# Dummy matmuls moved into the gaps of a fill, and one GpSimd addition put behind a sum: attention and gated FFN on one core

## The chip, the core and the metric

One core of a Trainium2 chip. The metric is the device time of one execution in microseconds; the time before is the median of five runs, 349.6 us. TensorE (PE) multiplies, VectorE (DVE), ScalarE (ACT) and GpSimd (POOL) work on what it leaves in PSUM and on SBUF; SyncE (SP) and GpSimd issue the DMAs. PSUM has eight banks, here one array `ps` of 128 x 8 x 512 fp32 values.

## What is computed

Hourglass attention over 8 batches x 8 heads, 576 positions, 64 per head, and then a gated FFN over the 4608 tokens:

```
q_d, k_d, v_d = means of q, k, v over 4 neighbouring positions
out_d  = softmax(scale * q_d k_d^T) v_d            # 144 x 144
local  = softmax(scale * q k^T where |i-j| < 4) v  # band of width 7
x      = repeat(out_d, 4) + local                  # 4608 tokens x 512
out    = (relu(x w_gate) * (x w_val)) w_out        # 512 -> 1536 -> 512
```

Inputs and output are fp32; the kernel computes in fp16 and sums in fp32.

## The kernel before, in words

Two heads make a pair; there are 32 pairs. The attention of a pair consists of its loads (q, k and v, cast to fp16 by POOL's DMAs), transposes of q and k, scores in 128-column blocks of the band and for the pooled keys, exponentials, masks, products with v, and a normalised sum into `xT`. The FFN takes 512 tokens at a time: `hg` and `hv` are the products with w_gate and w_val (four matmuls of 512 columns each, L639), `relu` (ACT) and `gate` (DVE) make `gT`, and the product with w_out is done by steps `p1` to `p7` (L724), a Strassen-like scheme that needs four sums of parts of `gT` on DVE (`sums`, L718: s1, s2, s3, s4; the 128-wide part `sumhi`, the rest `next`, and whole ones by `sum`). The last sum of an output unit is s4.

The order on each engine is written out by hand in three lists of tokens. `FRONT` is the fill: the first pairs are transposed on PE (`tr`, L364) and copied out (`ev`, by ACT or DVE, L378), v is pooled by PE (`vd`, L408, copied by `vc`), the scores are `s1` (L427, L438), their exponentials `ed` and `ex` (ACT), masks `ma` (DVE, L454), products `sd` (L475) and `su` (L487), the normalising steps on DVE `rd`, `td` (L504), `ru`, `tu` (L518), and the transposition into `xT` `xp` (L622, L624) with its copy `xe`. The last number of a token is its PSUM bank: `td/0/6` reads bank 6, and `ev/1/01A/7` reads bank 7. Loads are tokens too, so their place in the list is their place in POOL's queue. `ORDER` is one period of the body: four pairs and one FFN chunk; a token such as `v2/b/0` is kind, argument, half. `TAIL` ends the kernel without attention.

In the body POOL pools v: `v4` is the DMA load, `emit_v2` (L386) adds halves of it into an fp32 tile, `emit_v1` (L392) adds halves of that into `vd`. The step `after` (L994) copies one column of s4 to a scrap tile `seen`: POOL's queue stops there until that sum is done. It stands once in a period, as `after/3/0`. Transposes of q and k in the body are DMAs of SP (L344), issued with `scores`, followed by a reduction on DVE (L351).

`emit_warm` issues matmuls of zeros whose result nobody reads. Before, twelve of 512 columns come first (bank 7), and two groups of two, 248 columns each, in bank 6.

Of the kernel before, what the change touches and what calls it, by code (L numbers as in the profile page):

```python
# [16 lines left out]

FRONT = """
pads loadk/0 loadv/0 loadq/1 loadk/1 loadv/1 loadq/2 cast tr/0/2/4 loadk/2 ev/0/20V/4 tr/0/1/3
tr/0/0/2 ev/0/21V/4 ev/0/10A/3 vd/0/6 loadv/2 ev/0/11A/3 ev/0/01A/2 ev/0/00A/2 loadq/3 warm/2  # L20
tr/1/0/7 vc/0/6 s1/0/2 ev/1/00A/7 loadk/3 tr/1/2/1 ed/0/2 tr/1/1/0 ev/1/20V/1 ev/1/11A/0 loadv/3
sd/0/6 ev/1/21V/1 ev/1/10A/0 rd/0/6 ex/0/0/2 td/0/6 wg/0 warm/2 vd/1/6 ev/1/01A/7 ma/0/0
ex/0/1/2 s1/1/0 wv/0 ma/0/1 ed/1/0 ones/4 su/0/4 ex/1/1/0 ru/0/4 loadq/4 ex/1/0/0 tu/0/0/4
tr/2/1/2 tr/2/2/3 tu/0/1/4 ev/2/11A/2 tr/2/0/0 ev/2/10A/2 loadk/4 ev/2/21V/3 xp/0/0/4 ev/2/20V/3
ev/2/01A/0 xp/0/1/5 ev/2/00A/0 ma/1/0 loadv/4 vc/1/6 s1/2/0 ma/1/1 xe/0/0A/4 xe/0/1V/5 sd/1/6
ex/2/1/0 ones/5 su/1/4 rd/1/6 td/1/6 ed/2/0 ru/1/4 vd/2/6 loadq/5 tu/1/1/4 ex/2/0/0 tr/3/1/2
tu/1/0/4 tr/3/2/3 loadk/5 vc/2/6 tr/3/0/0 ev/3/20V/3 ev/3/10A/2 xp/1/1/5 sd/2/6 ev/3/21V/3
loadv/5 ev/3/01A/0 xe/1/1V/5 xp/1/0/4 ev/3/00A/0 ma/2/0 ev/3/11A/2 ma/2/1 xe/1/0A/4 s1/3/0 wg/1
rd/2/6 su/2/4 td/2/6 ed/3/0 ru/2/4 ex/3/0/0 tu/2/1/4 hv/0/0/7 wv/1 hv/0/1/7 tu/2/0/4 ex/3/1/0
vd/3/6 ma/3/0 ones/6 xp/2/1/5 vc/3/6 xp/2/0/4 ma/3/1 sd/3/6 xe/2/1V/5 xe/2/0A/4 loadq/6 tr/4/0/0  # L30
rd/3/6 su/3/4 td/3/6 tr/4/1/2 loadk/6 ru/3/4 hv/1/0/1 ev/4/11A/2 tu/3/0/4 hg/0/0/6 ev/4/10A/2
hg/0/1/6 tu/3/1/4 loadv/6 tr/4/2/3 ev/4/01A/0 ev/4/00A/0 xp/3/1/5 ev/4/21V/3 ev/4/20V/3 xp/3/0/4
wg/2 hv/0/2/7 xe/3/1V/5 xe/3/0A/4 hg/1/0/0 s1/4/2 wv/2 hv/0/3/7 ex/4/0/2 hv/1/1/1 loadq/7
# [75 lines left out]
ORDER = """  # L109
p/1/0 gate/5/1< scores/a/0 keep/1/0 gate/4/1< hg/0/0 exp/a0/0 sumhi/0/0 sumhi/1/0 exp/a1/0  # L110
hv/0/0 mask/a0/0 ed/a/0 mask/a1/0 p/2/0 next/0/1< relu/0/0 next/1/1< o/a00/0 o/a01/0 c11//0
o/a10/0 ln/a0/0 o/a11/0 sum/2/0 p/6/0 v/a/1 sum/3/0 p/5/0 keep/2/0 pool/b/0 v2/b/0 ln/a1/0 p/7/0
hg/2/0 keep/3/0 after/3/0 v1/a/1 inv/a/0 c22//0 p/4/0 gate/0/0 v2/a/0 p/3/0 xn/a1/0 c21//0 relu/2/0 hg/1/0
xn/a0/0 qk/a0/1 hv/2/0 relu/1/0 qk/a1/1 c12//0 xsum/a/0 scores/b/0 qk/a2/1 next/0/0 hv/1/0
exp/b0/0 v/b/0 exp/b1/0 hg/4/0 mask/b0/0 gate/1/0 v4/a/1 ed/b/0 hg/3/0 mask/b1/0 relu/4/0
gate/2/0 v1/b/0 o/b00/0 o/b01/0 o/b10/0 pool/a/0 ln/b0/0 o/b11/0 hv/4/0 v2/a/1 ln/b1/0 hv/3/0
# [53 lines left out]
def kernel(  # L170
# [34 lines left out]
    keep = ctx.enter_context(tc.tile_pool(name="keep", bufs=1))  # L205
# [15 lines left out]
    def ring(n, shape, dtype, name):  # L221
        return [keep.tile(shape, dtype, name=f"{name}{i}") for i in range(n)]
# [8 lines left out]
    v2 = [t[0:72] for t in v2full]  # L231
# [5 lines left out]
    ed = ring(2, [72, 2, 2 * SD + 64], FP16, "ed_")  # L237
    vd = ring(3, [72, 2, 192], FP16, "vd_")
# [3 lines left out]
    xn = keep.tile([128, 2, 360], FP16, name="xn")  # L242
# [7 lines left out]
    ps = psum.tile([128, 8, 512], FP32, name="ps")  # L250
# [45 lines left out]
    def emit_load_q1(hp, i):  # L296

        b, off = head_off(hp)
        src, dst, hh = (q, k)[i // 2], qk16[hp % NL][:, i // 2, :], i % 2
        if hp < NTP:  # L300
            if hh:
                return
            first = hp == 0 and src is q
            (nc.sync if first else nc.gpsimd).dma_start(
                (q32 if first else dst).rearrange("p (n d) -> p n d", d=64),
                _dap(src, off, [[D, 96], [NQ * D, 2 * NB], [1, D]]),
            )
            return
        nc.gpsimd.dma_start(  # L309
            dst.rearrange("p (j h d) -> p j h d", h=2, d=64)[:, :, hh, :],  # L310
            _dap(src, off + hh * S * D, [[D, 96], [NQ * D, NB], [1, D]]),
        )
# [182 lines left out]
    rd = ring(2, [72, 2, 2], FP32, "rd_")  # L495
    ru = ring(2, [96, 2, NB], FP32, "ru_")
# [310 lines left out]
            _dap(moe_w_out, 384 * i * D_MODEL, [[D_MODEL, 128], [128 * D_MODEL, 3], [1, D_MODEL]]),  # L807
        )

    def emit_warm(n, wide=False):  # L810
        for _ in range(n):
            nc.tensor.matmul(
                out=ps[:, 7, :] if wide else ps[:, 6, 264:512],
                lhsT=zero_sb[:, 0:128],
                rhs=zero_sb[:, 128 : 640 if wide else 376],
                start=True,
                stop=True,
            )
# [114 lines left out]
    def emit_tail_step(kind, arg, at):  # L933
        c, j = (int(at[0]), int(at[1])) if len(at) == 2 else (int(at or 0), 0)
        i = int(arg[0]) if arg else 0
        if kind in ("hg", "hv"):
            w = int(kind == "hv")
            bank = 4 + i if w else 2 * (j % 2) + i
            emit_h_mm(c, j + NK * i, w, range(4), ps[:, bank, :])
        elif kind == "relu":  # L940
            emit_relu(2 * j + i, ps[:, 2 * (j % 2) + i, :])
        elif kind == "gate":
            emit_gate(c, j + NK * i, 2 * j + i, ps[:, 4 + i, :])
        elif kind in ("gateg", "gateb"):
            nc.vector.scalar_tensor_tensor(
                out=gT[c % 2][:, j + NK * i, :],
                in0=block(c, j, 0).t[i],
                scalar=0.0,
                in1=ps[:, 4 + i, :] if kind == "gateg" else block(c, j, 1).t[i],
                op0=ALU.max,  # L950
                op1=ALU.mult,
            )
        elif kind == "xs":
            emit_xs(c, i)
        elif kind == "wg":
            emit_ws(0, i, 0, 768, nc.vector)
        elif kind == "wv":
            emit_ws(1, i, 192 * int(arg[1]), 192 * int(arg[1]) + 192, nc.gpsimd)
        elif kind in ("qg", "qv"):
            block(c, j, int(kind == "qv")).q(i)  # L960
        elif kind in ("keepg", "keepv"):
            block(c, j, int(kind == "keepv")).keep(i - 1)
        elif kind in ("tg", "tv"):
            block(c, j, int(kind == "tv")).out(arg)
        elif kind == "part":
            lo, hi = ((0, 3), (3, 5), (5, 6))[int(arg[1])]
            unit(c, j).sums(lo, hi, (i,))
        else:
            UNIT_STEPS[kind](unit(c, j), i)

    def emit_step(kind, arg, u, c):

        banks = (u, 1 - u)
        i = int(arg[-1]) if arg and arg[-1].isdigit() else 0
        if kind in H_STEPS:
            pp, jj = banks[i % 2], 6 * u + i
            if kind == "relu":
                emit_relu(i, pair(pp)[:, 0, :])
            elif kind == "gate":
                emit_gate(c, jj, i, pair(pp)[:, 1, :])  # L980
            else:
                w = int(kind == "hv")
                emit_h_mm(c, jj, w, range(4), pair(pp)[:, w, :])
        elif kind in UNIT_STEPS:
            UNIT_STEPS[kind](unit(c - 1, u), i)
        elif kind == "next":
            w = unit(c - 1, 1) if u == 0 else unit(c, 0)
            w.sums(0, NK if u == 0 else 5, (i,))
        else:
            PAIR_STEPS[kind](4 * c + 2 * u + LEAD + "ab".index(arg[0]), arg[1:])  # L990
# [45 lines left out]
    def emit_periods(c0, c1):  # L1036
        for base in range(c0, c1 + 2):
            for tok in ORDER.split():
                c = base + {">": 1, "<": -1}.get(tok[-1], 0)
                kind, arg, u = tok.rstrip("<>").split("/")  # L1040
                if c == c1 - 1 and base > c:
                    continue
                if c0 <= c < c1 or c == c0 - 1 and f"{kind}/{arg}/{u}" in LATE:
                    emit_step(kind, arg, int(u), c)

    def emit_front(tok):
        kind, *a = tok.split("/")
        if "@" in tok:
            emit_step(kind, a[0], *map(int, a[1].split("@")))
        else:  # L1050
            FRONT_STEPS[kind](*[int(x) if x.isdigit() else x for x in a])

    FRONT_STEPS = {
        "pads": emit_pads,
        "cast": lambda: nc.scalar.copy(out=qk16[0][:, 0, :], in_=q32),
        "warm": emit_warm,
        "loadq": lambda p: emit_load_q1(p, 0),
        "loadk": lambda p: emit_load_q1(p, 2),
# [37 lines left out]
    with tc.manual_schedule(engines={ET.PE, ET.DVE, ET.Activation, ET.SP, ET.Pool}):  # L1096
        nc.scalar.dma_start(cst_sb[:, 960:1080], cst_dr[:, 960:1080])
        emit_load_q1(0, 0)
        nc.sync.dma_start(cst_sb[:, 0:960], cst_dr[:, 0:960])
        nc.sync.dma_start(cst_sb[:, 1080:1368], cst_dr[:, 1080:1368])  # L1100
        emit_warm(12, True)
        for tok in FRONT.split():
            emit_front(tok)
        emit_periods(PS // 4, (NP - LEAD) // 4)
        for tok in TAIL.split():
            kind, arg, *at = tok.split("/")
            if at:
                emit_tail_step(kind, arg, at[0])
            else:
                emit_step(kind, arg, 1, NCH - 3)  # L1110
# [30 lines left out]
```

## Time and profile before

| | us |
|---|---|
| median of 5 runs | 349.6 |
| lowest, highest | 347.19, 351.98 |
| profiled execution, its own time | 349.6 |
| its span, first to last instruction | 347.8 |

The mean granted TensorE clock of the profiled execution is 0.979 of full. In the page, a row of digits gives 40 equal slices of the span, 8.7 us each, with the busy share in tenths; PEclk is the granted clock in tenths. In a timeline a row gives start, length, engine, line, operation and tiles, xN for N merged instructions, and in brackets the idle time before it with what ended it. In a table by stage, each engine's busy microseconds are followed by its number of instructions. [...]

### The profile page before, as it was taken

What the parts mean: (1) busy time and instruction counts of PE and PEld (TensorE: products, weight loads), DVE (VectorE), ACT (ScalarE), POOL (GpSimd) and SP (SyncE); (2) the same over time, 40 slices, a digit from 0 to 9 for tenths busy, and PEclk for the clock granted to TensorE, in tenths of its full rate; (3) what the DMA queues carried; (4) which work ended last, traced back from release to release, by engine and by line L of the source; (5) the groups of instructions that cost most, each with busy time, mean ns of one, the idle gap of its engine ahead of it and who ended that gap; (6) DMA issues with size and microseconds to landing.
All of it is one profiled execution on the core that took longest, in us unless ns stands there. A gap on an engine that the chain in (4) does not pass through costs nothing.

```text
span 347.8 us, 8224 instructions
## 1 busy us (share of the span) xinstructions
PE 339.2 (98%) x3210; PEld 218.1 (63%) x3210; DVE 296.3 (85%) x546; ACT 218.5 (63%) x423; POOL 182.2 (52%) x232
## 2 busy tenths in 40 slices
PE   7799999999999999999999999999999999999996
PEld 3676555757566655665566656665666557767685
DVE  5566659999899999999999999999999798786892
ACT  3766876777766776767667765776767634344222
POOL 8986547796789894977587696950300000000000
PEclk9759999999999999999999999999999999999999
DMA  9999999999999999799969995992000001001023
GB/s 145 165 170 187 185 189 154 151 177 148 148 170 156 140 163 142 95 141 151 150 75 144 164 152 62 156 151 70 30 32 33 30 0 47 32 31 47 32 74 108
DMA packets 167975, 40.02 MB, mean 115 GB/s; under 512 B 149857, under 2 KB 164865, under 8 KB 167937
## 3 DMA queue, kind: packets, MB, share of 16 engines
q0 software_dynamic: 132160, 22.63, 93.4%
q1 hardware_dynamic: 35632, 16.84, 27.7%
q8 instruction: 25, 0.41, 0.5%
q14 instruction: 14, 0.11, 0.1%
q10 hardware_dynamic: 144, 0.03, 0.1%
HBM read 45.86 MB, written 9.44 MB: 159 GB/s over the span
## 4 chain that ended last, share of the span: by engine, by line
PE 88%; DVE 5%; DMA 2%; ACT 2%; issue 1%; POOL 1%; DVEq 0%; ACTq 0%; POOLq 0%
PE ps L639 46%; PE ps L724 22%; PE ps L905 4%; PE ps L585 3%; PE ps L438 2%; PE ps L427 2%; PE ps L364 2%; DMA qk<-in_k_dram 2%; PE ps L593 2%; PE ps L408 1%; DVE xn L612 1%; ACT rden L603 1%; DVE ee L454 1%; DVE xo L718 1%; PE ps L622 1%
## 5 line engine op out<-in xcount | busy, mean ns | idle before, releaser
L639 PE MATMUL ps<-xT,wv_sb 128*128 128x512 f16 x432 | 109.5, 380 | 0.0
L639 PE MATMUL ps<-xT,wg_sb 128*128 128x512 f16 x352 | 88.4, 380 | 0.0
L648 ACT ACTIVATE r<-ps 128x512 f16<-128x512 f32 x88 | 52.0, 596 | 31.4 <-PE ps L639 28.8
L651 DVE TENSOR_TENSOR gT<-r,ps 128x512 f16<-128x512 f16 x88 | 58.8, 681 | 7.7 <-PE ps L639 4.9
L639 PEld LDWEIGHTS <-wv_sb 128*128 128x128 f16 x432 | 40.5, 98 | 39.7
L639 PEld LDWEIGHTS <-wg_sb 128*128 128x128 f16 x352 | 32.6, 98 | 32.3 <-issue 0.2
L612 DVE TENSOR_TENSOR xn<-ps,rden 64x720 f16<-64x720 f32 x48 | 43.5, 905 | 4.1 <-ACT rden L608 2.7
L603 ACT ACTIVATE rden<-ps 64x720 f32<-64x720 f32 x48 | 36.7, 765 | 14.6 <-PE ps L593 13.5
L448 ACT ACTIVATE ee<-ps 112x576 f16<-112x576 f32 x64 | 38.8, 648 | 6.6 <-PE ps L438 5.6
L309 POOL DMA_DIRECT2D qk<-in_q_dram x46 | 33.6, 735 | 11.5 <-DMA qk<-in_k_dram 3.2
L724 PEld LDWEIGHTS <-gT 128*128 128x128 f16 x324 | 31.5, 98 | 9.0
L454 DVE TENSOR_TENSOR ee<-ee,cst_sb 112x576 f16<-112x576 f16 x64 | 31.9, 519 | 5.8 <-ACT ee L448 5.2
L309 POOL DMA_DIRECT2D qk<-in_k_dram x46 | 33.7, 736 | 4.6 <-DMA v<-in_v_dram 2.2
L334 POOL DMA_DIRECT2D vw<-in_v_dram x30 | 28.7, 955 | 9.2 <-PE ps L724 4.4
L724 PEld LDWEIGHTS <-xo 128*128 128x128 f16 x288 | 27.4, 98 | 7.7 <-DVE xo L718 0.3
L351 DVE TENSOR_REDUCE qkd<-qkT 128x288 f16<-128x1152 f16 x23 | 30.9, 1343 | 0.0
L758 ACT COPY q<-ps 128x256 f32<-128x256 f32 x45 | 16.8, 373 | 21.5 <-PE ps L724 20.7
L724 PE MATMUL ps<-wo_sb,gT 128*128 128x256 f16 x216 | 28.0, 273 | 0.0
L724 PE MATMUL ps<-wt,xo 128*128 128x256 f16 x216 | 27.7, 273 | 0.2 <-DVE xo L718 0.2
L386 POOL TENSOR_TENSOR v<-v 72x512 f32<-72x512 f16 x21 | 25.0, 1190 | 2.8 <-DMA v<-in_v_dram 2.2
L915 ACT COPY vw<-ps 128x256 f32<-128x256 f32 x30 | 10.8, 374 | 20.7 <-PE ps L905 13.8
L571 DVE TENSOR_TENSOR xT<-xn 128x576 f16<-128x576 f16 x28 | 22.8, 814 | 0.5
(108 smaller groups left out, 562.9 us busy)
## 6 DMA issues: line engine op xcount, KB each, us to landing
out_dram<-y_sb SPq DMA_DIRECT2D x24, 256.0 KB, 3.4
vw<-in_v_dram POOLq DMA_DIRECT2D x30, 168.0 KB, 7.0
qk<-in_q_dram POOLq DMA_DIRECT2D x46, 72.0 KB, 6.5
qk<-in_k_dram POOLq DMA_DIRECT2D x46, 72.0 KB, 6.5
v<-in_v_dram POOLq DMA_DIRECT2D x21, 144.0 KB, 7.1
out_dram<-y_sb SPq DMA_DIRECT2D x22, 128.0 KB, 1.7
wg_sb<-in_moe_w_gate_dram POOLq DMA_DIRECT2D x4, 384.0 KB, 10.3
wv_sb<-in_moe_w_val_dram POOLq DMA_DIRECT2D x4, 384.0 KB, 10.9
```

The source lines that it names most:

```text
L309: nc.gpsimd.dma_start(dst.rearrange("p (j h d) -> p j h d", h=2, d=64)[:, :, hh, :], _dap(src, off + hh * S * D, [[D, 96], [NQ * D, NB], [ ...
L334: nc.gpsimd.dma_start(t, _dap(v, base, [[D, WK], [NQ * D, n], [1, D]]))
L351: nc.vector.tensor_reduce(out=qkd[hp % 2].rearrange("p i t -> p (i t)"), in_=qkT[hp % 4][:, 0 : 2 * S].rearrange("p (t f) -> p t f", f=4), ...
L386: nc.gpsimd.tensor_tensor(out=m, in0=t[:, :, 0:128], in1=t[:, :, 128:256], op=ALU.add)
L448: nc.scalar.activation(out=o, in_=ps[0:WK, p0 + 2 * g : p0 + 2 * g + 2, 0:288], func=AF.Exp, scale=scale)
L454: nc.vector.tensor_tensor(out=o, in0=o, in1=_sap(masks_sb, (0, WK), 288 * g, [[0, 2], [1, 288]]), op=ALU.mult,)
L603: nc.scalar.activation(out=rden[lo : lo + 64], in_=ps[de : de + 64, 4 + 2 * hh : 6 + 2 * hh, 0:360], func=AF.Ln)
L612: nc.vector.tensor_tensor(out=xn[lo : lo + 64], in0=ps[lo : lo + 64, 4 + 2 * hh : 6 + 2 * hh, 0:360], in1=rden[lo : lo + 64], op=ALU.mult,)
L639: nc.tensor.matmul(out=out, lhsT=w[:, kk, bass.ts(jj, 128)], rhs=xT[:, kk, c * TCH : (c + 1) * TCH], start=(kk == 0), stop=(kk == 3),)
L648: nc.scalar.activation(out=r1[j % 3], in_=h1, func=AF.Relu)
L651: nc.vector.tensor_tensor(out=gT[c % 2][:, jj, :], in0=r1[j % 3], in1=h2, op=ALU.mult)
L724: nc.tensor.matmul(out=out, lhsT=left[:, i, :], rhs=right[i], start=(first and i == 0), stop=(i == NK - 1), skip_group_check=True,)
```

## The change

Two edits. In the fill the dummies get a bank as a second argument, and there are more of them: 14 wide ones first, then groups of 5, 5, 5, 1, 3 and 4 of 248 columns, in banks 6, 7, 7, 7, 7 and 1. The second group stands behind `vd/1` and the copy of bank 7, where it stood ahead of `vd/1`. In the body `v2/b/0` (one addition of L386 per period) moves from behind `pool/b/0` to behind `after/3/0`. The order of ACT, DVE and SP is the same; on POOL only the addition and the `seen` copy change places, in five periods; PE has 21 more matmuls, with their weight loads.

```diff
 FRONT = """
...
-tr/0/0/2 ev/0/21V/4 ev/0/10A/3 vd/0/6 loadv/2 ev/0/11A/3 ev/0/01A/2 ev/0/00A/2 loadq/3 warm/2
+tr/0/0/2 ev/0/21V/4 ev/0/10A/3 vd/0/6 loadv/2 ev/0/11A/3 ev/0/01A/2 ev/0/00A/2 loadq/3 warm/5/6
 tr/1/0/7 vc/0/6 s1/0/2 ev/1/00A/7 loadk/3 tr/1/2/1 ed/0/2 tr/1/1/0 ev/1/20V/1 ev/1/11A/0 loadv/3
-sd/0/6 ev/1/21V/1 ev/1/10A/0 rd/0/6 ex/0/0/2 td/0/6 wg/0 warm/2 vd/1/6 ev/1/01A/7 ma/0/0
+sd/0/6 ev/1/21V/1 ev/1/10A/0 rd/0/6 ex/0/0/2 td/0/6 wg/0 vd/1/6 ev/1/01A/7 warm/5/7 ma/0/0
 ex/0/1/2 s1/1/0 wv/0 ma/0/1 ed/1/0 ones/4 su/0/4 ex/1/1/0 ru/0/4 loadq/4 ex/1/0/0 tu/0/0/4
-tr/2/1/2 tr/2/2/3 tu/0/1/4 ...
+warm/5/7 tr/2/1/2 tr/2/2/3 tu/0/1/4 ...
-... ma/1/0 loadv/4 vc/1/6 s1/2/0 ma/1/1 ...
+... ma/1/0 loadv/4 vc/1/6 warm/1/7 s1/2/0 ma/1/1 ...
-ex/2/1/0 ones/5 su/1/4 rd/1/6 td/1/6 ed/2/0 ru/1/4 vd/2/6 loadq/5 ...
+ex/2/1/0 ones/5 su/1/4 rd/1/6 td/1/6 ed/2/0 ru/1/4 warm/3/7 vd/2/6 loadq/5 ...
...
-vd/3/6 ma/3/0 ones/6 xp/2/1/5 vc/3/6 ...
+vd/3/6 ma/3/0 ones/6 warm/4/1 xp/2/1/5 vc/3/6 ...
...
 ORDER = """
...
-... keep/2/0 pool/b/0 v2/b/0 ln/a1/0 p/7/0
-hg/2/0 keep/3/0 after/3/0 v1/a/1 inv/a/0 ...
+... keep/2/0 pool/b/0 ln/a1/0 p/7/0
+hg/2/0 keep/3/0 after/3/0 v2/b/0 v1/a/1 inv/a/0 ...
...
-    def emit_warm(n, wide=False):
+    def emit_warm(n, bank=7, wide=False):
         for _ in range(n):
             nc.tensor.matmul(
-                out=ps[:, 7, :] if wide else ps[:, 6, 264:512],
+                out=ps[:, 7, :] if wide else ps[:, bank, 264:512],
                 lhsT=zero_sb[:, 0:128],
                 rhs=zero_sb[:, 128 : 640 if wide else 376],
...
-        emit_warm(12, True)
+        emit_warm(14, wide=True)
```

## The prediction

> **What bounds the kernel now.** I read the page first, then the busy time by stage, then the timelines of TensorE and of VectorE, then the same around GpSimd's `seen` copy.
>
> ```profile
> PE 339.2 (98%) x3210; PEld 218.1 (63%) x3210; DVE 296.3 (85%) x546; ACT 218.5 (63%) x423; POOL 182.2 (52%) x232
> ...
> PE   7799999999999999999999999999999999999996
> ...
> DVE  5566659999899999999999999999999798786892
> ...
> PEclk9759999999999999999999999999999999999999
> ```
>
> PE is full from the third slice (17 us) to the last, and the granted clock is below full in slices two and three alone. From 95 to 237 us I compared each matmul's start with the start before it: what its columns do not explain is 0.97 to 1.6 us in each period of 35.4 us. So the body is bound by PE, and a microsecond won in the fill arrives at the end, if nothing else becomes late. The fill by stage (columns: PE, PEld, DVE, ACT, POOL busy, then the clock and DMA):
>
> ```profile
> 5.60:8.90 3.30, 2.01 (x35) 1.15 (x33) 0.95 (x4) 0.84 (x4) 3.30 (x5) 1.00 2.42 155
> 9.00:12.30 3.30, 2.14 (x50) 1.65 (x51) 1.58 (x5) 3.05 (x9) 3.30 (x5) 1.00 2.43 155
> 12.40:15.70 3.30, 2.80 (x46) 2.42 (x46) 1.49 (x5) 2.01 (x4) 3.30 (x5) 0.50 2.39 160
> 15.80:19.10 3.30, 3.30 (x53) 2.68 (x49) 2.07 (x6) 2.31 (x7) 3.30 (x5) 0.50 1.41 200
> 19.20:22.50 3.30, 3.17 (x47) 2.61 (x45) 2.57 (x7) 2.33 (x7) 2.26 (x4) 0.50 2.24 162
> 22.70:26.00 3.30, 3.30 (x43) 2.38 (x41) 2.34 (x7) 2.09 (x6) 3.30 (x5) 0.50 2.32 163
> 26.10:29.40 3.30, 3.11 (x55) 2.12 (x54) 3.06 (x10) 1.52 (x6) 2.04 (x4) 1.00 1.37 202
> ```
>
> The clock is halved for four equal stretches, from 12.39 to 26.04 us. There PE is busy while DVE and ACT are some 65% busy: the half clock sets the pace. (At the very start the record shows 1.00, but the first dummies stand 427 ns apart, later 512-column matmuls 216 ns: half rate until 5.56.)
>
> ```profile
> 8.51 0.38 PE L812 MATMUL ps<-zero_sb 128*128 128x248 f16 x2
> 9.23 0.40 PE L364 MATMUL ps<-cst_sb,qk 96*64 96x120 f16 x8 [0.34 <-DMA qk<-in_q_dram]
> ...
> 12.09 0.37 PE L812 MATMUL ps<-zero_sb 128*128 128x248 f16 x2 [0.80 <-DVE xo L504]
> 12.30 0.75 PE L408 MATMUL ps<-vw,cst_sb 112*128 112x128 f16 x6
> ...
> 15.20 1.41 PE L364 MATMUL ps<-cst_sb,qk 96*64 96x120 f16 x24 [0.50 <-ACT ee L448]
> ```
>
> The second pair of dummies waits for `td` (they share bank 6), so it comes after the gap that it might have filled.
>
> [...] Weighting each matmul's streaming time by the rows and columns used, I get 0.44 of a full array for 5.56 to 8.97 (clock kept) and 0.34 for 8.97 to 12.39 (clock halved); in the four half-rate windows 0.60, 0.64, 0.64 (not restored) and 0.78 (restored). [...]
>
> **The change part by part.**
>
> *Dummies up to 12.09.* Two more 512-wide ones cost 2 x 0.216 to 0.427, 0.43 to 0.85, inside the wait of 1.27 before the first transposes at 7.41. The first short group grows from 2 to 5 at 0.104 (248 columns): 0.52 from 8.51 to 9.03, inside the wait that ends at 9.23. Both cost nothing; uncovered, they would cost their length.
>
> *Second group.* `vd/1` now comes first: it starts at 12.09 when `td` is done, takes six times 0.056, ends at 12.43; five dummies follow to 12.95 (their bank 7 is free at 12.13, after ACT's copy). So the scores of pair 1 start at 12.98 as before, but at full clock take 0.42 in place of 0.78.
>
> *Third group.* `su/0` needs the masks (13.18) and runs from 13.42 to 13.80; five dummies to 14.32. The transposes of pair 2 wait for ACT: `ed` 0.65 and `ee` 0.55 after the scores, so they start at 14.70, not 15.20. The dummies end inside that wait: 0.50 won.
>
> *From there to 26.6* VectorE sets the pace. Its own rows:
>
> ```profile
> 14.99 1.02 DVE L518 TENSOR_TENSOR xo<-ps,ru 96x384 f16<-96x384 f32 x2
> ...
> 20.13 1.02 DVE L518 TENSOR_TENSOR xo<-ps,ru 96x384 f16<-96x384 f32 x2
> ...
> 25.55 1.02 DVE L518 TENSOR_TENSOR xo<-ps,ru 96x384 f16<-96x384 f32 x2
> ```
>
> Cycles of 5.14 and 5.42. VectorE's work per pair: copies 0.25 + 0.56, masks 0.82, x out 0.46, `rd` 0.18, `td` 0.42, `ru` 0.23, `tu` 1.02: 3.94. At full clock PE delivers each input in time but for small waits: I take 4.17 and 3.95. `tu` then ends at 15.18, 19.35, 23.30 in place of 16.01, 21.15, 26.57: 3.3 us won. The 1, 3 and 4 later dummies (0.10, 0.31, 0.41) lie in PE's waits for ACT and for `td`, `tu`. After 26.04 both run at full clock in the same order, so 3.3 stays. Bounds: 1.9 if the clock is still lost (below), 4.0 if DVE's waits vanish too.
>
> *Loads* must not stop it. In the trace the first w_val slice lands at 21.04 and is first used at 24.99: margin 4.0 against 3.4 won by then; pair 4's q 5.6, the second w_gate slice 5.8, the v of pair 9 5.2, the first DMA transpose 6.2 ahead of its reduction. All hold, the first by 0.6.
>
> *GpSimd's first v addition.* Five times it moves behind `seen`, which already waits for the last sum: no new wait, 1.17 us of work goes from ahead of it to behind it. Behind it stand `v1`, the next `v2`, then q, k, v and v4 loads (each 0.73 to 0.94 of POOL), and with them, through the landed tiles, SP's transposes. All come 1.17 later in periods two to four (in the first `seen` waited for nothing; in the fifth no load follows). POOL then idles 1.07 and 3.02 by 158.8, 1.67 and 1.76 by 195, 2.23 by 229, which takes the delay up, and the transposes land over 6 us ahead. Cost: nothing; without that cover 3 x 1.17 = 3.5. The gain is in one place:
>
> ```profile
> 207.63 1.17 POOL L386 TENSOR_TENSOR v<-v 72x512 f32<-72x512 f16 x1
> 212.15 0.19 POOL L994 COPY seen<-xo 128x1 f16<-128x1 f16 x1 [3.35 <-DVE xo L718]
> ```
> ```profile
> 207.81 1.08 DVE L718 TENSOR_TENSOR xo<-gT 128x128 f16<-128x128 f16 x1
> 208.93 0.22 DVE L718 TENSOR_TENSOR xo<-xo,gT 128x128 f16<-128x128 f16 x1
> ```
>
> A sum of 0.22 took 1.08 beside the addition, and PE lost 0.20 and 0.35 at 209.4 and 210.5 waiting for it. In the other four the addition lay beside work that it slowed by 0.09 or not at all. So 0 to 0.55; behind `seen` it may meet other work, so I take 0.4.
>
> **Sum** against the profiled execution: span 347.8 - 3.3 - 0.4 = 344.1, plus the 1.8 around it: 345.9. That execution took 349.6, which is also the median of the five runs.
>
> **The rivals.** *Clock still lost* (18%). The longest gap, 11.13 to 12.09, gets nothing: the second group is queued behind `vd/1`, which waits for the same `td`. [...] Then vd/1 and the dummies run at half rate, the transposes of pair 2 start 0.9 late at 16.1; but that window holds over 0.8, the clock is back at 15.8, and 8.6 us later (as above from 14.70 to 23.31) stands 24.7 against 26.62: 1.9 won, 347.3. *Loads take it back* (8%): for the small margin of w_val and saturated DMA; against: the other margins. Gain about 1.6: 347.6. *Slower* (8%): the half clock lasts as before, to 26, and dummies are paid at half rate, 0.207 each. Place: 12.4 to 20. Price: scores 0.6 late, the third group 0.5 beyond its wait, 0.4 for the next four: 1.5, with the second edit 350.7. It decides if the window after the loss stays under what restores it; 0.84 against 0.64 speaks against. *POOL's delay reaches PE* (4%): 345.9 + up to 3.5 = 349.4.
>
> **How the numbers follow.** Clock held: 62%, 345.9, own range 344.8 to 347.0. The rest as above. 344.6 to 349.0 leaves out the slower case and a little at each end. About 1% is what a measurement can tell from no change; that bound is 346.1, just above my number, so a little over half of the first case lies below it and, of the others, some hundredths: faster 0.40. Slower (over 353.1) is the slower case with a further loss: 0.06. Same: 0.54.
>
> **What would show it.** Right: clock 1.00 from about 6 to the end, pair 2's transposes near 14.7, `tu` near 19.3 and 23.3, hg's first matmul near 25.5, periods still near 35.4, the 128x128 sums all 0.22. Wrong: a half clock after 12 us, PE waits with a DMA behind them between 22 and 75 us, or PE losing more than 1.6 in a period, waiting for xn, xT or masks slowed by the moved addition.

## The result and the profile after

| | before | with the change |
|---|---|---|
| median, us | 347.43 (77 runs) | 345.79 (40 runs) |
| lowest, highest, us | 345.44, 357.31 | 344.13, 347.74 |
| profiled execution, its span, us | 349.6, 347.8 | 344.8, 343.0 |
| its mean granted clock | 0.979 | 1.000 |

The ratio is 0.9954, 95% interval 0.9939 to 0.9969: faster by about 0.5%, which is within the 1% that the prediction counted as "same". The changed kernel came out where it was forecast (345.9, measured 345.79); the kernel before did not: its median is 347.4, not 349.6, so by the medians 1.6 us were gained and not 3.7. Runs over 1.5% above the fastest of their kernel are left out of the ratio; their clock is not on record here, but in the sets below, where it is, every run of before as long as these had 0.981 or less.

The two profiled executions differ by more than either figure, 4.8 us. The changed one is a good run of its kernel, 1.0 below its median, so it is in part luck that the median met the forecast so closely.

The page of the changed kernel has lost its slow clock:

```profile
PE 336.0 (98%) x3231; PEld 215.9 (63%) x3231; DVE 292.1 (85%) x546; ACT 218.2 (64%) x423; POOL 182.0 (53%) x232
...
PE   8899999999999999999999999999999999999996
...
PEclk9999999999999999999999999999999999999999
```

The same stages as in the prediction, columns as there (PE, PEld, DVE, ACT, POOL, clock, DMA):

```profile
9.00:12.30 3.30, 2.30 (x55) 1.89 (x56) 1.69 (x5) 2.87 (x8) 3.30 (x5) 1.00 2.43 155
12.40:15.70 3.30, 3.03 (x64) 2.36 (x63) 1.99 (x6) 2.26 (x6) 3.30 (x5) 1.00 2.38 161
15.80:19.10 3.30, 3.15 (x76) 2.64 (x75) 3.04 (x9) 3.20 (x9) 3.30 (x5) 1.00 1.34 202
19.20:22.50 3.30, 3.12 (x61) 2.40 (x56) 3.13 (x11) 2.99 (x8) 2.67 (x5) 1.00 2.33 162
```

From 15.8 on VectorE and ScalarE are busy for 3.0 to 3.2 of 3.3 us, where they had 2.1 to 2.6: with the full clock they set the pace. TensorE's timeline shows the groups of dummies (L812) and what follows each:

```profile
7.94 0.69 PE L812 MATMUL ps<-zero_sb 128*128 128x248 f16 x5
9.00 0.40 PE L364 MATMUL ps<-cst_sb,qk 96*64 96x120 f16 x8 [0.37 <-DMA qk<-in_q_dram]
...
11.87 0.49 PE L408 MATMUL ps<-vw,cst_sb 112*128 112x128 f16 x6 [0.80 <-DVE xo L504]
12.20 0.69 PE L812 MATMUL ps<-zero_sb 128*128 128x248 f16 x5
12.82 0.25 PE L427 MATMUL ps<-qkd 64*72 64x144 f16 x2
...
13.71 0.69 PE L812 MATMUL ps<-zero_sb 128*128 128x248 f16 x5
14.67 0.94 PE L364 MATMUL ps<-cst_sb,qk 96*64 96x120 f16 x24 [0.27 <-ACT ee L448]
```

The second group stands between the pooling (L408) and the scores (L427), with no wait after it: it is on the path. After the third PE still waits, 0.27 for `ee`: that one is covered.

### The profile page after: what moved, and what is told of

Its sections match the earlier page's. It is cut to its first block, busy times and chain, and to the rows that moved or that the text cites. A ratio compares the mean times of both kernels' runs of the same rounds, so it can differ in the third digit from the quotient of the medians.

```text
span 343.0 us, 8266 instructions
## 1 busy us (share of the span) xinstructions
PE 336.0 (98%) x3231; PEld 215.9 (63%) x3231; DVE 292.1 (85%) x546; ACT 218.2 (64%) x423; POOL 182.0 (53%) x232
## 4 chain that ended last, share of the span: by engine, by line
PE 93%; DMA 2%; ACT 1%; DVE 1%; POOL 1%; issue 1%; DVEq 0%; ACTq 0%; POOLq 0%
PE ps L639 50%; PE ps L724 23%; PE ps L905 4%; PE ps L585 4%; PE ps L438 2%; PE ps L427 2%; PE ps L593 2%; DMA qk<-in_q_dram 2%; PE ps L364 1%; PE ps L408 1%; DMA out_dram<-y_sb 0%; PE ps L549 0%; PE ps L528 0%; ACT ed L462 0%; PE ps L475 0%
## 5 line engine op out<-in xcount | busy, mean ns | idle before, releaser
L454 DVE TENSOR_TENSOR ee<-ee,cst_sb 112x576 f16<-112x576 f16 x64 | 29.4, 477 | 5.8 <-ACT ee L448 5.1
L386 POOL TENSOR_TENSOR v<-v 72x512 f32<-72x512 f16 x21 | 25.4, 1209 | 2.0 <-DMA v<-in_v_dram 1.4
L608 ACT ACTIVATE rden<-rden 128x720 f32<-128x720 f32 x28 | 22.5, 804 | 0.7
```

The lines of the kernel that those rows point to most:

```text
L386: nc.gpsimd.tensor_tensor(out=m, in0=t[:, :, 0:128], in1=t[:, :, 128:256], op=ALU.add)
L454: nc.vector.tensor_tensor(out=o, in0=o, in1=_sap(masks_sb, (0, WK), 288 * g, [[0, 2], [1, 288]]), op=ALU.mult,)
```

## The experiments

Theory after the result: the kernel before loses its clock in some executions and keeps it in others, and the profiled run of before was a bad one. Rivals: the loss is in every run alike; the order of waits, not the activity, was the cure; all of the gain belongs to one of the edits. In what follows "full clock" means runs with a mean clock of 0.999 or more. A "stretch" (a "window" in the recorded texts) is 3.41 us, a quarter of the 13.65 that the first profiled run of before spent at half clock (12.39 to 26.04). The mean clocks of the 137 runs of before in the sets below fit this length: below 0.998 they lie within 0.002 of 0.995, 0.985, 0.980, 0.976, 0.971, 0.966 and 0.962, and half rate for 3.41 us takes 0.005 from the mean clock of 346 us. A share of a full array is an estimate from the matmul records, worked out as in the prediction.

**The kernel before once more, and the dummies without their length.**

> The kernel before once more, to see the granted clock of each of its runs. [...] Rival (the loss is in every run alike and the profiled run was typical): all runs near 0.979 and the spread of times has nothing to do with the clock.

```diff
(e3) -                out=ps[:, 7, :] if wide else ps[:, bank, 264:512],
     +                out=ps[:, 7, :] if wide else ps[:, bank, 264:280],
     -                rhs=zero_sb[:, 128 : 640 if wide else 376],
     +                rhs=zero_sb[:, 128 : 640 if wide else 144],
```

> Both edits, with the dummies in the same places, banks and order, but the 23 short ones 16 columns wide in place of 248, so that they keep their waits and take almost none of PE's time. Theory (it is the activity that counts): the clock is lost again, mean clock 0.98 to 0.99 in most runs, and the time rises to that of the addition alone or above it, 346.5 to 349. Rival (what the change did was the order of waits and the banks, the second group behind the pooling): as with both edits, 345.8, clock 1.0.

Of the six runs of the kernel before, three had the full clock (344.92 to 345.84) and three 0.98 to 0.985 (348.76 to 350.11). The profiled one had the full clock, with four dummies, and its span is 343.1, as long as the changed kernel's 343.0:

```profile
8.50:11.80 3.30, 2.37 (x56) 1.84 (x54) 1.74 (x5) 2.95 (x7) 3.30 (x5) 1.00 2.44 155
11.90:15.20 3.30, 2.50 (x61) 2.12 (x60) 2.38 (x7) 2.71 (x7) 3.30 (x6) 1.00 2.43 157
15.30:18.60 3.30, 2.75 (x71) 2.37 (x72) 3.03 (x9) 3.20 (x9) 3.30 (x5) 1.00 1.42 200
```

Where a stretch begins in a run that keeps its clock is not shown; I put them at 8.42, 11.84 and so on (an estimate), half a microsecond from those of the run that was studied first. With dummies of 16 columns four runs of six had 0.98 and 347.57 to 349.8, two the full clock and 345.11 and 345.91. Same banks, same order, same waits, and only TensorE's work is less, and none of the 41 runs of the changed kernel with its result is below 0.995: it is the activity that kept the clock. Its profiled run loses it at 13.3, and the row after the loss reads 0.50:

```profile
9.90:13.20 3.30, 2.12 (x53) 1.96 (x53) 2.21 (x7) 2.63 (x8) 3.30 (x5) 1.00 2.45 160
13.40:16.60 3.20, 2.90 (x43) 2.49 (x44) 2.60 (x7) 2.59 (x8) 3.20 (x5) 0.50 2.05 172
```

**Each edit alone, twice, and both again.**

```diff
(fill alone)   ORDER as before
(order alone)  FRONT, emit_warm and the first emit_warm call as before
```

> Only the dummies of the fill are changed; the GpSimd addition stays where it was. Theory: clock 1.0 in nearly all runs; 3.6 us gained over a before run with four half-rate windows, but only about 0.5 to 1.0 over the median of before, ratio 0.997 to 0.9985; the sum of 128 columns still takes about 1.08 us in one period. Rival (all of the gain is the fill's): ratio 0.9954 as with both edits. Rival (all of it is the addition's): ratio 1.000.

> Only the GpSimd addition is moved; the fill is as before. Theory: no clock change against before, runs with clock below 1.0 stay; the 128-column sums all 0.22 us and PE loses nothing by them: 0.6 to 1.2 us gained, ratio 0.9965 to 0.9985. Rival (all of the gain is the fill's): ratio 1.000. Rival (loads that come 1.17 us later in three periods reach PE): over 1.003.

> Both edits once more, as the measure for the other three on the same chip. Theory: clock 1.0, or 0.995 in a few runs, 344.5 to 347, median 345.7; the runs of the kernel before fall apart into some with clock 0.999 or 1.0 near 345.6 and some with 0.98 or less at 348.7 and above. Rival (the change is also faster where the clock is kept anyway): before runs with full clock lie more than 1 us above this kernel.

> The fill's dummies alone, once more with more runs, to size each edit among runs with full clock. Theory (the second group costs 0.5 on the path, the move of the addition gains 0.55 elsewhere): full-clock runs 0.5 above the full-clock runs of before on this chip, and 0.4 to 0.6 above those with both edits. Rival (the dummies gain even where the clock is kept): full-clock runs below those of before.

> The moved addition alone, once more. Theory: full-clock runs 0.4 to 0.6 below the full-clock runs of before; runs with clock of 0.98 or less stay, in the same share as before (about 4 in 10). Rival: no difference among full-clock runs.

| us | median of all (runs) | full clock, median (runs) | before on the same chip: all, full clock | ratio, 95% |
|---|---|---|---|---|
| fill alone | 346.15 (6) | 346.13 (5) | 349.69 (11), 345.63 (5) | 0.9995, 0.9946 to 1.0045 |
| order alone | 345.59 (6) | 345.06 (5) | the same | 0.9972, 0.9915 to 1.0029 |
| both again | 345.61 (21) | 345.60 (17) | 347.49 (75), 346.54 (35) | 0.9946, 0.9922 to 0.997 |
| fill alone again | 346.55 (22) | 346.45 (21) | 347.76 (51), 346.36 (25) | 0.9983, 0.9959 to 1.0007 |
| order alone again | 347.47 (22) | 346.06 (11) | the same | 0.9997, 0.9963 to 1.0031 |

With the fill's dummies no run of these 49 had less than 0.99, nor did any of the 120 others in this document that have them in full length; with the order alone 12 of 28 did, as before (61 of 137). So the clock belongs to the fill alone. Where the clock is full anyway, the fill gains nothing: 0.5 and 0.1 above before. The moved addition stands 0.6 and 0.3 below before there. None of these four differences is clear of the scatter (full-clock runs of one kernel spread over 1 to 4 us), and the medians alone do not show that the moved addition gains; the profiles do, as told below. Both together stand 0.9 below before with full clock, which is clear of the scatter and more than the parts add up to; why is open.

The profiled run of "both again" is the case that the prediction gave 18%. The 3.41 us before the loss, put at 8.47 to 11.88, held 0.31 of a full array, and the next ran at half rate:

```profile
8.50:11.80 3.30, 2.11 (x52) 1.48 (x50) 1.39 (x5) 2.79 (x8) 3.30 (x5) 1.00 2.44 155
11.90:15.20 3.30, 3.30 (x41) 2.53 (x40) 0.65 (x2) 1.10 (x3) 3.30 (x6) 0.50 2.44 158
15.30:18.60 3.30, 3.19 (x75) 2.65 (x74) 3.09 (x9) 3.11 (x9) 3.30 (x5) 1.00 1.47 198
```

There the dummies themselves run at half rate (the second group's row 1.24 us long in place of 0.69), fill that stretch to 0.85, and the clock is back in the row from 15.3, after one stretch instead of four.

**Where the second group stands, and its length.**

```diff
(e5) -sd/0/6 ev/1/21V/1 ev/1/10A/0 ... vd/1/6 ev/1/01A/7 warm/5/7 ma/0/0
     +sd/0/6 ev/1/21V/1 warm/6/1 ev/1/10A/0 ... vd/1/6 ev/1/01A/7 ma/0/0
(e6) -vd/1/6 ev/1/01A/7 warm/5/7 ma/0/0
     +vd/1/6 ev/1/01A/7 warm/15/7 ma/0/0
(e10) as e5, with ORDER as before
```

> Both edits, but the second group of dummies (five behind the pooling of pair 1) becomes six in bank 1, ahead of that pooling, in PE's wait of 0.8 us for td. Theory: the five cost 0.45 to 0.52 us on the path where they stood and nothing in the wait, so the scores of pair 1 start 0.5 earlier and the time falls by 0.4 to 0.5, to 345.2 to 345.3; the window before 12.4 us is fuller by 0.15, so that no run loses the clock there. Rival (the group cost nothing because the scores wait for something else then): the same time as with both edits.

> Both edits, with the second group 15 dummies long in place of 5. Theory (it lies on the path): ten more at 0.104 us delay the scores of pair 1 by 1.04 us and the end by 0.9 to 1.1, median 346.7. Rival (VectorE or the loads set the pace of the fill, PE has room): under 0.3 later, 345.7 to 346.0.

> The addition as before, the fill with its second group in the wait ahead of the pooling (bank 1). Theory: clock 0.995 or more in all runs, and full-clock runs 0.5 below those of the fill alone, so level with the full-clock runs of before or 0.2 below (before's own pair of dummies cost 0.21 there). Rival (where the group stands is of no account): level with the fill alone.

Group in the gap (e5): 345.03 (22 runs) beside 345.61 with both edits and 347.49 before on that chip; ratio to before 0.993, interval 0.9905 to 0.9955. It has the lowest median here; its 0.6 below both edits is at the edge of the scatter. Fifteen dummies (e6): 347.02 in all, and with full clock 346.95, 1.35 above both edits where 0.9 to 1.1 was expected. TensorE with the group in the gap, then with fifteen:

```profile
10.62 0.80 PE L812 MATMUL ps<-zero_sb 128*128 128x248 f16 x6
11.43 0.50 PE L408 MATMUL ps<-vw,cst_sb 112*128 112x128 f16 x6
11.86 0.25 PE L427 MATMUL ps<-qkd 64*72 64x144 f16 x2
```
```profile
11.74 0.49 PE L408 MATMUL ps<-vw,cst_sb 112*128 112x128 f16 x6 [0.80 <-DVE xo L504]
12.07 1.75 PE L812 MATMUL ps<-zero_sb 128*128 128x248 f16 x15
13.75 0.25 PE L427 MATMUL ps<-qkd 64*72 64x144 f16 x2
```

Neighbouring rows overlap (11.43 and 0.50 of length against 11.86), so I go by the starts: from pooling to scores it is 0.43, 0.95 (with both edits) and 2.01 us: 0.52 for five, 1.06 for ten more, 0.104 to 0.106 each. The theory holds in place and, within the fill, in price; the further 0.3 of e6 at the end is within the scatter. One of 22 runs of e5 still had a clock below 0.999 (347.85), so "no run" was too much.

The gap fill without the moved addition (e10) missed its number: the clock was full in 14 of 14, but the median is 346.87, level with the fill alone (346.45) and not 0.5 below, as the rival had it. Its one profile shows what happened in that run: the lead of 4.8 over the first profiled run of before shrank to 3.0 after 88.7, when POOL, late behind its DMAs (waits of 1.06 us to 80.42 and of 0.85 to 85.85), put three additions beside VectorE's `xT` copy and masks (POOL, VectorE, TensorE):

```profile
86.59 1.17 POOL L386 TENSOR_TENSOR v<-v 72x512 f32<-72x512 f16 x1
87.72 1.26 POOL L392 TENSOR_TENSOR vd<-v 72x256 f16<-72x256 f32 x1
89.06 1.25 POOL L386 TENSOR_TENSOR v<-v 72x512 f32<-72x512 f16 x1
```
```profile
86.64 1.75 DVE L571 TENSOR_TENSOR xT<-xn 128x576 f16<-128x576 f16 x1
88.32 2.30 DVE L454 TENSOR_TENSOR ee<-ee,cst_sb 112x576 f16<-112x576 f16 x2
```
```profile
90.76 0.29 PE L585 MATMUL ps<-ee,vw 112*128 112x96 f16 x3 [1.64 <-DVE ee L454]
```

The masks usually take 0.82 for two, `xT` 0.75; PE lost 1.80 there. These additions lie ahead of the first one that the change moves, and the first run of the order alone lost 1.74 at the same place with the addition moved: the edits do not decide it. Measured against PE's course in the first profiled run of before, the profiled executions lost between 67 and 112 us: nothing in four (that run itself, the changed kernel, e5 and e7), and 0.3 to 1.9 in the nine others, nearly all of it at two places. It is the largest difference between executions with full clock. What makes POOL late in some runs is open. So is why e10 and e5, which differ in the moved addition alone, lie 1.8 apart (on different chips, whose full-clock medians of before are 346.36 and 346.54): the place that the addition spoils accounts for 0.55.

**The addition put beside the sums on purpose.**

```diff
-... keep/3/0 after/3/0 v2/b/0 v1/a/1 ...
+... keep/3/0 after/2/0 v2/b/0 after/3/0 v1/a/1 ...
-... in_=w.s4[:, NK - 1, 127:128]),
+... in_=w.s4[:, NK - 1, 127:128] if i == 3 else w.s2[:, 0, 0:1]),
```

> Both edits, but the GpSimd addition waits for the second sum and not for the last one, so that in each of five periods it runs while VectorE does the third and the fourth. Theory (the addition slows a sum that lies beside it, and PE waits where VectorE is late): the third or fourth sum takes 1.1 us and not 0.55 in most periods, and 0.3 to 0.6 us of it reach PE in each, 346.7 to 348.5 in all. Rival (VectorE has that much room; the loss in one period of the profiled run before was chance): sums 1.1 us long but under 0.3 us in all, 345.7 to 346.0.

`after/2` makes POOL wait for the second sum in place of the last. The median is 346.07 (22 runs; full clock 346.05), 0.45 above both edits, a difference within the scatter. The profile shows it: the third sum takes 1.5 us in four periods; here is one, with the fourth sum after it:

```profile
207.12 1.52 DVE L718 TENSOR_TENSOR xo<-gT 128x768 f16<-128x768 f16 x1
208.56 0.55 DVE L718 TENSOR_TENSOR xo<-gT,xo 128x768 f16<-128x768 f16 x1
```

Only in this period does PE fall back for it, by 0.41. Both theories were half wrong: the sums suffer more than expected (1.0 us each), and in three of four places that microsecond does not reach PE.

## Why the prediction was right and where it was not

*The sum's starting point was wrong, and this is what halved the gain.* "That execution took 349.6, which is also the median of the five runs": I took its four half-rate stretches for the usual case and read the spread from 347.19 to 351.98 as more or fewer of them. Over 137 runs of before beside the experiments, 65 had the full clock, 11 between 0.99 and 0.998, and 61 less. Sorted by the half-rate stretches that the mean clock amounts to (3.41 us each), with six more runs of the copy: none, 346.5; four, 349.7; five, 351.2; six, 354.4; seven, 355.9. (Out of order are one stretch, 349.1 in six runs, and three, 348.0 in four; why is open.) The mean of the 137 is 349.3, of both edits 345.8: in the mean over all runs 3.5 us are gained, near the 3.7 forecast (in the runs of the result itself 349.1 and 345.8, so 3.2). The median sees 1.6 to 1.9, since half the runs of before had nothing to lose. I gave the changed kernel a chance of losing its clock and the kernel before no chance of keeping it; the spread of its five runs should have told me to.

*The 3.3 for the fill was right:* at 28 us PE leads the profiled run of before by 3.6. It was not free of cost: where the kernel before kept its clock (the second run of before and both of the order alone), PE leads by 4.4 to 4.6 there, and the three profiled fills with these dummies and a full clock, 3.6 to 4.3. By the medians four half-rate stretches cost 3.2 (349.7 less 346.5), less than in the traces; the full-clock runs profiled lose part of their lead later.

*The fill, step by step.* Forecast and measured in the profile: pair 2's transposes 14.70, 14.67; `tu` ends at 15.18, 19.35, 23.30, measured 15.19, 19.23, 22.98; first `hg` 25.5, 25.24. VectorE set the pace, and its rows show the three ends:

```profile
14.17 1.02 DVE L518 TENSOR_TENSOR xo<-ps,ru 96x384 f16<-96x384 f32 x2
...
18.21 1.02 DVE L518 TENSOR_TENSOR xo<-ps,ru 96x384 f16<-96x384 f32 x2
...
21.96 1.02 DVE L518 TENSOR_TENSOR xo<-ps,ru 96x384 f16<-96x384 f32 x2
```

By 24 us PE leads the run of before by 3.4 and from 28 to 112 us by 3.6. The second group's 0.52 on the path is what I had counted. The two wide dummies were not wholly inside their wait in this run: the first transposes, at 6.84, no longer wait for their load but follow the dummies at once, while in the full-clock run of before they start on landing at 6.35. At 9.00 PE still waits 0.37 for its next load, which takes that delay up.

*The shares of a full array*, 0.34 where the clock was lost and 0.44 where it was kept, 0.64 where it did not come back and 0.78 where it did, held their order in every profile with a clock record (the first of the fill alone has none) and came closer, all of them estimates worked out as in the prediction: lost at 0.30 to 0.34 in four stretches, kept at 0.36 to 0.44 in eight; not restored at 0.68, restored at 0.75. The 3.3 went by these shares of one profile. But I had not tried them on the kernel before with other places of the stretches: put at 8.42 and 11.84, its stretches hold 0.39 and 0.40 and keep the clock. The 18% for "clock still lost" was an estimate of mine from the places that a stretch can take, and no run shows how these are spread; the return after one stretch in its sum, at 15.8, no run had shown either, and "both again" then showed it, with 0.50 from 11.9 and 1.00 from 15.3. The 18% was fair: 7 of 61 runs of the two measurements of the change lost one stretch, median 347.0 (forecast 347.3), and none lost more.

*The slower case* did not occur: with the dummies at half rate the clock was back after one stretch ("both again", 0.50 in the row from 11.9 and 1.00 in that from 15.3), as argued against it.

*The addition.* The place was right, and the size near it: 0.4 was forecast, and the sum that it slowed accounts for 0.55 (0.19 and 0.36). All profiles agree. In four of the five with the addition where it was, the small sum at 204 to 208 us took 0.64 to 1.08 beside it; in the fifth, the fill alone again, the addition slowed the masks that follow (1.77 in place of 0.82), and PE came out 0.69 late in place of 0.55:

```profile
205.38 1.35 POOL L386 TENSOR_TENSOR v<-v 72x512 f32<-72x512 f16 x1
```
```profile
205.28 1.77 DVE L454 TENSOR_TENSOR ee<-ee,cst_sb 112x576 f16<-112x576 f16 x2
207.11 0.29 PE L585 MATMUL ps<-ee,vw 112*128 112x96 f16 x3 [0.26 <-DVE ee L454]
```

In all eight with the addition moved that sum is clean, and PE gains the 0.55 against the first run of before. In the changed kernel the addition follows `seen` (VectorE, then POOL):

```profile
203.40 0.22 DVE L718 TENSOR_TENSOR xo<-gT 128x128 f16<-128x128 f16 x1
203.65 0.22 DVE L718 TENSOR_TENSOR xo<-xo,gT 128x128 f16<-128x128 f16 x1
```
```profile
206.89 0.19 POOL L994 COPY seen<-xo 128x1 f16<-128x1 f16 x1 [4.79 <-PE ps L724]
207.04 1.15 POOL L386 TENSOR_TENSOR v<-v 72x512 f32<-72x512 f16 x1
```

PE's lead also grew by 0.34 at 164, where masks were slow in the first run of before (1.72 for two) and less so here (0.99), and by 0.18 at 200. The moved addition did neither: the first grew as much in the second run of before and in both runs of the fill alone, and the second as much in the later of these. Loads 1.17 later reached nobody in this run: from 95 to 237 us PE loses nothing against the run of before.

*Loads* did not stop the fill. But "loads take it back" exists in another form: late loads make POOL late, and POOL's additions then lie beside masks (88.7 us above, 2.30 for two masks). It strikes runs with and without the edits.

## What to carry to other kernels

Look at the granted clock of several executions of the kernel before, not of one: here the same fill, with the same wait of 0.80 us, was followed by 13.65 us at half clock in one profiled run and by none in another, 61 of 137 runs had a mean clock under 0.99, and the price of a change is then the chance times the loss. Put dummies where PE already waits, in a bank that is free there, and ahead of the instruction that waits; here five behind it cost 0.52 us, their full length. A GpSimd addition beside a VectorE sum made the sum longer in many of the places where they met in these profiles (0.22 became 0.64 to 1.08, 0.55 became 1.52), not in all, and cost time only where TensorE was about to need the sum (0.55 and 0.41 us).

## What the runs showed of the hardware

In these profiles the changes between half and full rate went with the streaming time weighted by rows and columns in stretches of 3.41 us (an estimate, the figures in brackets), not with PE's busy time. The prediction's first two rows show it for the loss: from 5.60 to 8.90 PE was busy for 2.01 of 3.30 us and the clock was kept (0.44), from 9.00 to 12.30 for 2.14 and it was lost (0.34). For the return, of two stretches at half rate with PE busy throughout, one was not enough (0.64, the prediction's row from 15.80) and one was (0.85, the row of "both again" from 11.90). Nor was this one enough, of the run with 16-column dummies (0.68):

```profile
16.80:20.10 3.30, 3.24 (x57) 2.83 (x53) 1.85 (x5) 2.40 (x5) 3.30 (x5) 0.50 1.56 191
```

Beyond four half-rate stretches each further one cost about 2.1 us (355.9 for seven against 349.7 for four), more than the 1.7 that half rate takes from PE in 3.41 us; none of the profiles is of such a run, and the cause is open.
